# Weights' parts of a second MoE re-timed between blocks, and its first stores given to GpSimd

## The chip, the cores and the metric

The kernel runs on one core of one Trainium2 chip. The metric is the device time of one execution in microseconds. Engines are named as in the profile: PE is TensorE, DVE VectorE, ACT ScalarE, POOL GpSimd, SP SyncE; PEld is TensorE's loading of weights.

## The reference, cut to what matters

Three stages follow each other: a chunked local attention with memory tokens, a gated MoE, and a second MoE that sums four experts. The change lies in the second MoE:

```python
def _moe2_ref(x, domain_probs, w1, w2):          # x 1536x512, w1 4x512x1024, w2 4x1024x512
    p = domain_probs / (domain_probs.sum(-1, keepdims=True) + 1e-09)
    out = np.zeros((N, D), dtype=np.float32)
    for e in range(E):
        h = np.maximum(x @ w1[e], 0.0)
        out += p[:, e:e + 1] * (h @ w2[e])
    return out
```

## The kernel before, in words

**Numbers in two parts.** Matrices are multiplied as float32r in a high and a low part. ScalarE casts a matrix to its high part (`hi`, a copy), VectorE subtracts that from the matrix and gives the low part (`lo`), and `mm3` (lines 177 to 180) issues three matmuls: high by high, high by low, low by high.

**Seven products instead of eight.** In the second MoE both products, x by w1 and h by w2, are done on 2 x 2 quarters with seven products each and sums of quarters in between. So the weights of a group of half an expert's columns need four sums on VectorE (`s1` to `s4` for w1, `t4` to `t7` for w2, lines 282 and 327), seven casts on ScalarE (lines 272, 333) and seven low parts on VectorE (lines 278, 339). The sums overwrite the raw weights in place, so their order against casts and low parts is bound: a cast of a sum comes after it, and a sum that overwrites a quarter comes after the low part that reads it.

**Blocks.** There are eight groups (four experts, two halves each) and two halves of the tokens, so 16 blocks; blocks 2g and 2g+1 share group g's weights. Blocks 0 and 1 are plain in their second product (`plain_block`, `unit`, `o_part`): `flush` (line 546) scales a result on ScalarE (line 550) into one of four staging buffers `st`, and SP stores it plainly to the output (line 551), six stores of 256 KB per block. Blocks 2 to 15 (`block`) use seven products twice. Their results go through eight smaller buffers `st` and are added to the output by accumulating DMAs from GpSimd (line 662); `stage` (line 677, ScalarE), `second` (line 685, VectorE) and `c12` (line 694, ScalarE) read the results out of PSUM.

**The order of work.** The program is recorded in the order of the code (`manual_schedule`), and every engine takes its instructions in that order. In `block`, `product(n, u, m, ps, first)` is one of the seven products for unit u (six matmuls of 384 columns); `held` copies it to a small tile s on ScalarE (line 464), `total` adds two on VectorE (line 619, v<-a, v<-b, v<-e), the function `hi` makes the high part of h (lines 606, 608) and `lo` the low one (lines 613, 616), `s_sum` the sums of h (line 622), and `q` multiplies h with w2. The last third of each block's second products (`third`, `seventh`, `sixth`, `fourth`, `fifth`, in `left`) is run within the first third of the next block, between its products. `third(2)` adds to the PSUM tile B[2], which `fifth` has VectorE read (line 685) just before.

**Weights for the next group.** `w1_prep` and `w2_prep` return lists of steps. `block` puts them in `hooks` (lines 717 to 727), and `hook(n)` emits the next n steps at fixed places between products, so that a group's preparation is spread over the two blocks before it and the first of its own. In the lists a sum is followed by its cast and then by the cast's low part:

```python
        return [
            both(start, hi(1, "b11")), both(lo(1, "b11"), hi(2, "b21"), t5), both(lo(2, "b21"), t7),
            hi(7, "b12"), both(lo(7, "b12"), t6, hi(6, "b12")), both(lo(6, "b12"), t4, hi(4, "b21")),
            both(lo(4, "b21"), hi(5, "b11")), both(lo(5, "b11"), hi(3, "b22")),
            both(lo(3, "b22"), lambda: raw2_load(n + 1))]
```

**SP's queue** issues, in order, the loads of raw weights (lines 230, 239), the writes of y's seven parts to memory and their loads back (lines 370, 373, 768 KB each), and the plain stores (line 551).

Of the kernel before, what the change touches and what calls it, by code (L numbers as in the profile page):

```python
# [27 lines left out]
DM, DFF = 512, 1536  # L28
# [41 lines left out]
def fused_kernel(ctx: ExitStack, tc: tile.TileContext, kq0, kq1, kvw, kvc, vl, w_g, w_v, w_o, w_1, w_2, probs, out):  # L70
# [136 lines left out]
    raw1_t, raw2_t = [], []  # L207
# [50 lines left out]
    def w1_prep(n):  # L258

        t = {}  # L260

        def start():
            raw1_load(n)
            r0, r1 = raw1[n]
            t.update(a11=r0[:, :2], a12=r0[:, 2:], a21=r1[:, :2], a22=r1[:, 2:])
            ops1[n] = {}

        def hi(m, a):
            def do():
                s = slot("w")  # L270
                ops1[n][m] = s, quarters(s)
                nc.scalar.copy(out=ops1[n][m][1][:, 0], in_=t[a])
            return do

        def lo(m, a):
            def do():
                w = ops1[n][m][1]
                nc.vector.tensor_tensor(out=w[:, 1], in0=t[a], in1=f32(w[:, 0]), op=ALU.subtract)
            return do

        def comb(dst, a, b, op):
            return lambda: nc.vector.tensor_tensor(out=t[dst], in0=t[a], in1=t[b], op=op)


        s1 = comb("a22", "a21", "a22", ALU.add)
        s3 = comb("a21", "a11", "a21", ALU.subtract)
        s2 = comb("a11", "a22", "a11", ALU.subtract)
        s4 = comb("a12", "a12", "a11", ALU.subtract)
        return [
            both(start, hi(4, "a22"), hi(1, "a11")), both(lo(4, "a22"), s1),  # L290
            both(hi(2, "a12"), lo(1, "a11"), s3, s2), both(lo(2, "a12"), s4), hi(7, "a21"),
            both(hi(6, "a11"), lo(7, "a21")), lo(6, "a11"),
            both(hi(5, "a22"), hi(3, "a12")), lo(5, "a22"), both(lo(3, "a12"), lambda: raw1_load(n + 1))]
# [21 lines left out]

    def w2_prep(n):

        b = {}

        def start():  # L320
            raw2_load(n)
            r0, r1 = raw2s[n]
            b.update(b11=r0[:, :, :DH], b12=r0[:, :, DH:], b21=r1[:, :, :DH], b22=r1[:, :, DH:])
            ops3[n] = {}

        def comb(dst, x, y, op):
            return lambda: nc.vector.tensor_tensor(out=b[dst], in0=b[x], in1=b[y], op=op)

        def hi(m, x):
            def do():  # L330
                s = slot("w2")
                ops3[n][m] = s, quarters(s)
                nc.scalar.copy(out=ops3[n][m][1][:, :, 0], in_=b[x])  # L333
            return do

        def lo(m, x):
            def do():
                w = ops3[n][m][1]
                nc.vector.tensor_tensor(out=w[:, :, 1], in0=b[x], in1=f32(w[:, :, 0]), op=ALU.subtract)  # L339
            return do  # L340


        t5 = comb("b11", "b12", "b11", ALU.subtract)
        t7 = comb("b12", "b22", "b12", ALU.subtract)
        t6 = comb("b12", "b11", "b22", ALU.subtract)
        t4 = comb("b21", "b21", "b12", ALU.add)
        return [
            both(start, hi(1, "b11")), both(lo(1, "b11"), hi(2, "b21"), t5), both(lo(2, "b21"), t7),
            hi(7, "b12"), both(lo(7, "b12"), t6, hi(6, "b12")), both(lo(6, "b12"), t4, hi(4, "b21")),
            both(lo(4, "b21"), hi(5, "b11")), both(lo(5, "b11"), hi(3, "b22")),  # L350
            both(lo(3, "b22"), lambda: raw2_load(n + 1))]
# [76 lines left out]
    def second_block():  # L428
# [17 lines left out]
        def small(name, n):  # L446
            return sp.tile([128, HT], F32, tag=name, bufs=n, name=name)
# [897 lines left out]
```

## Time and profile before

| | |
|---|---|
| runs | 842.0, 843.4, 845.23 us (median 843.4) |
| the profiled execution | 843.81 us, its span 842.0 us |
| busy: PE | 827.6 us (98% of the span) |
| busy: PEld | 764.1 us (91%) |
| busy: DVE | 536.4 us (64%) |
| busy: ACT | 440.9 us (52%) |
| busy: POOL | 157.2 us (19%) |
| granted PE clock | 1.0 in every slice |
| chain that ended last | PE 65%, issue 16%, POOL 7%, DVE 5%, DMA 4%, ACT 3% |

The profiled execution's own time stands 1.8 us above its span, for what lies before the first and after the last instruction. Matmuls are pipelined, so that one starts while the one before is still running; PE's busy time is the union of them. The second MoE begins at about 345 us: plain blocks 0 and 1 take until about 410 us, and the other fourteen blocks about 30 us each. In the timelines a row with "xN" stands for N instructions in a row, and what stands in brackets is the idle time of the engine before it and what ended it.

### The profile page before, as it was taken

To read this page: it belongs to the slowest core of one execution; us is meant where nothing else is said; L and a number is where in the kernel's file an instruction comes from. 1 tells how busy PE (TensorE), PEld (TensorE's weight loads), DVE (VectorE), ACT (ScalarE), POOL (GpSimd) and SP (SyncE) were. 2 spreads that over 40 slices of the span, in tenths; PEclk is the share of its full clock that TensorE was granted. 3 is DMA by queue.
4 is the path that set the end of the run, shared out by engine and by line. 5 is a ranking of instruction groups with operands and counts; after the bars stand their busy time and mean duration, and the time that the engine had idled before them with its cause. 6 is when DMAs were issued, how large, how long until landed. Compare 5 with 4: busy or idle time off the path is not lost.

```text
span 842.0 us, 14479 instructions
## 1 busy us (share of the span) xinstructions
PE 827.6 (98%) x5566; PEld 764.1 (91%) x5566; DVE 536.4 (64%) x1041; ACT 440.9 (52%) x953; POOL 157.2 (19%) x182
## 2 busy tenths in 40 slices
PE   9999999999999999999999999999999999999998
PEld 6899998888888888888899999999999999999997
DVE  7753346342342229456588688788787787887847
ACT  5864454332232335445466666565665666666642
POOL 3220000000000000000032432333343243243231
PEclk9999999999999999999999999999999999999999
DMA  9984043111200005381593894893994994994783
GB/s 346 342 274 157 20 132 134 66 52 49 76 26 1 0 1 242 121 336 52 175 306 36 133 345 51 165 312 38 186 289 46 216 261 48 245 231 52 248 172 76
DMA packets 48614, 127.48 MB, mean 151 GB/s; under 512 B 5648, under 2 KB 27552, under 8 KB 48544
## 3 DMA queue, kind: packets, MB, share of 16 engines
q1 hardware_dynamic: 25616, 105.67, 34.8%
q0 software_dynamic: 22928, 20.88, 19.5%
q8 instruction: 44, 0.72, 0.3%
q14 instruction: 26, 0.21, 0.1%
HBM read 90.35 MB, written 36.18 MB: 150 GB/s over the span
## 4 chain that ended last, share of the span: by engine, by line
PE 65%; issue 16%; POOL 7%; DVE 5%; DMA 4%; ACT 3%; SPq 0%; POOLq 0%; ACTq 0%; DVEq 0%
POOL out_dram L662 7%; PE pv L178 4%; PE pv L180 4%; PE pv L179 4%; PE pg L179 4%; PE pg L178 4%; PE pb L178 4%; PE pb L179 4%; PE pb L180 4%; PE pg L180 4%; DMA out_dram<-st 3%; PE b L178 2%; PE b L179 2%; PE b L180 2%; PE B L178 2%
## 5 line engine op out<-in xcount | busy, mean ns | idle before, releaser
L662 POOL DMA_DIRECT2D out_dram<-st x159 | 137.3, 953 | 623.9 <-DVE st L685 599.1
L178 PE MATMUL b<-yo,w_s 128*128 128x384 f32 x256 | 87.2, 341 | 3.6 <-ACT s L464 2.9
L179 PE MATMUL b<-yo,w_s 128*128 128x384 f32 x256 | 86.5, 338 | 0.0
L180 PE MATMUL b<-yo,w_s 128*128 128x384 f32 x256 | 86.4, 337 | 0.0
L1086 ACT ACTIVATE sg<-pg 128x512 f32<-128x512 f32 x36 | 21.5, 598 | 84.2 <-PE pg L180 84.2
L622 DVE SCALAR_TENSOR_TENSOR v<-v 128x384 f32<-128x384 f32 x112 | 62.0, 553 | 4.6 <-ACT v L774 3.6
L178 PE MATMUL pv<-xs,w_v 128*128 128x384 f32 (+1 forms) x176 | 64.2, 365 | 0.0
L180 PE MATMUL pv<-xs,w_v 128*128 128x384 f32 (+1 forms) x176 | 61.7, 351 | 0.0
L179 PE MATMUL pv<-xs,w_v 128*128 128x384 f32 (+1 forms) x176 | 61.5, 349 | 0.0
L180 PE MATMUL pg<-xs,w_g 128*128 128x512 f32 x144 | 56.0, 389 | 0.0
L179 PE MATMUL pg<-xs,w_g 128*128 128x512 f32 x144 | 56.0, 389 | 0.0
L178 PE MATMUL pb<-hl,w_o 128*128 128x512 f32 x144 | 56.0, 389 | 0.0
L179 PE MATMUL pb<-hl,w_o 128*128 128x512 f32 x144 | 56.0, 389 | 0.0
L180 PE MATMUL pb<-hl,w_o 128*128 128x512 f32 x144 | 56.0, 389 | 0.0
L178 PE MATMUL pg<-xs,w_g 128*128 128x512 f32 x144 | 56.0, 389 | 0.0
L117 DVE TENSOR_TENSOR hl<-g,hl 128x512 fp32r<-128x512 f32 x36 | 24.7, 690 | 48.5 <-ACT hl L116 48.5
L464 ACT COPY s<-b 128x384 f32<-128x384 f32 x64 | 30.8, 481 | 46.1 <-PE b L180 44.6
L178 PEld LDWEIGHTS b<-yo,w_s 128*128 128x128 f32 x256 | 48.2, 188 | 6.1 <-ACT s L464 4.8
L178 PE MATMUL B<-w_s,h 128*128 128x256 f32 x171 | 48.9, 286 | 2.2 <-DVE st L685 2.2
L116 ACT CAST hl<-g 128x512 fp32r<-128x512 f32 x36 | 22.2, 623 | 54.8 <-PE pb L180 54.8
L339 DVE TENSOR_TENSOR w_s<-raw,w_s 128x512 fp32r<-128x512 f32 x49 | 33.7, 689 | 25.1 <-ACT w_s L333 25.1
L178 PE MATMUL B<-w_s,hx 128*128 128x256 f32 x165 | 47.0, 285 | 2.4 <-DVE st L685 2.4
(281 smaller groups left out, 2457.9 us busy)
## 6 DMA issues: line engine op xcount, KB each, us to landing
yo<-kept_y SPq DMA_DIRECT2D x49, 768.0 KB, 9.2
out_dram<-st POOLq DMA_DIRECT2D x159, 128.0 KB, 4.4
raw<-in_w_dram SPq DMA_DIRECT2D x32, 512.0 KB, 6.5
kept_y<-yo SPq DMA_DIRECT2D x14, 768.0 KB, 3.8
kv<-in_kvc_dram SPq DMA_DIRECT2D x20, 483.0 KB, 5.8
raw<-in_w_v_dram SPq DMA_DIRECT2D x12, 512.0 KB, 6.7
raw<-in_w_g_dram SPq DMA_DIRECT2D x12, 512.0 KB, 5.5
raw<-in_w_o_dram SPq DMA_DIRECT2D x12, 512.0 KB, 3.3
```

What stands on the lines that cost most here:

```text
L116: nc.scalar.copy(out=hi, in_=src)
L117: nc.vector.tensor_tensor(out=lo, in0=src, in1=f32(hi), op=ALU.subtract)
L178: nc.tensor.matmul(out=ps, lhsT=w_hi, rhs=r_hi, start=first, stop=False, skip_group_check=more)
L179: nc.tensor.matmul(out=ps, lhsT=w_hi, rhs=r_lo, start=False, stop=False, skip_group_check=more)
L180: nc.tensor.matmul(out=ps, lhsT=w_lo, rhs=r_hi, start=False, stop=last, skip_group_check=more)
L339: nc.vector.tensor_tensor(out=w[:, :, 1], in0=b[x], in1=f32(w[:, :, 0]), op=ALU.subtract)
L464: nc.scalar.copy(out=s, in_=ps[:, :HT])
L622: nc.vector.scalar_tensor_tensor(out=out, in0=x, scalar=0.0, in1=y, op0=ALU.max, op1=op)
L662: nc.gpsimd.dma_start(out=out_of(n, t, cols_of(dh)), in_=st, accum_op=ALU.add)
L1086: nc.scalar.activation(out=sg, in_=ps, func=AF.Sigmoid)
```

## The change

1. **Steps by name.** `w1_prep` and `w2_prep` now give a dictionary of single steps: "h4" is the cast of part 4, "l4" its low part, "s1" to "s7" the sums (s5, s7, s6, s4 are the former t5, t7, t6, t4), "x" the load of the next group's raw weights. `block` names at each place the steps to be emitted there, and `hooks` isn't used there any more.
2. **Order in a block.** In an even block l5, l3, x of w1 and l7, s6, s4 of w2 come after the first product, then the casts h6 and h4 with their low parts after product 7, the casts h5 and h3 alone between the next products, and l5 and l3 of w2 in mid-block (after product 3 of unit 0, and after product 7 of unit 1). In an odd block w1's first parts and sums stand as before, h1 and h2 of w2 are cast in the first third, and l1, then s5 and l2 come in mid-block. At the end of an odd block stand the casts h5 and h3 of w1, the sum s7 and the cast h7 of w2; at the end of an even block the casts h4, h1 and h2 of w1.
3. **`fifth` before a low part.** `do("5")` is called ahead of `lo(n, 0, 1, c11, True)` instead of behind it.
4. **Plain blocks.** In block 0 all four sums of y's second half come first, and `hook(2)` between the units is gone. In block 1 the cast h6 of w2 comes one step later (at the end of unit 1, behind s4).
5. **Plain stores.** `flush` issues its store on GpSimd's queue.

No instruction is added or left out; there are as many of each kind on PE, DVE and ACT.

```diff
+        def steps(of, sums):
+            do = {f"h{m}": hi(m, a) for m, a in of.items()}
+            do.update({f"l{m}": lo(m, a) for m, a in of.items()})
+            do.update({k: comb(*v) for k, v in sums.items()})
+            do["x"] = lambda: load(n + 1)
+            return do
...
+    def w1_do(g, steps):
+        if g < n_grp:
+            if g not in pre1:
+                pre1[g] = w1_prep(g)
+            for k in steps.split():
+                pre1[g][k]()
...
-            nc.sync.dma_start(out=out_of(n, tt, slice(0, DM)), in_=st)
+            nc.gpsimd.dma_start(out=out_of(n, tt, slice(0, DM)), in_=st)
...
-                thooks.extend(sums)
+                for do_sum in sums:
+                    do_sum()
             else:
-                env["w2"] = w2_prep(1)
-                thooks.extend(env["w2"][:6])
+                thooks.extend(each(w2_do, 1, "h1", "l1 h2 s5", "l2 s7", "h7", "l7 s6", "s4 h6", "l6 h4"))
             fin0 = unit(n, 0, prev)
-            if n == 0:
-                hook(2)
...
             product(n, 0, 1, b, True)
             s1 = held(b)
+            if odd:
+                w1_do(g + 1, "l4 s1 l1 s3 s2 l2 s4")
+            elif late:
+                w1_do(g, "l5 l3 x")
+                w2_do(g, "l7 s6 s4")
...
-            hook(2)
+            if odd:
+                w1_do(g + 1, "h7 l7 h6 l6")
+            else:
+                w2_do(g, "h6 l6 h4 l4" if late else "l4 h5 h3")
             product(n, 0, 6, b, False)
             s2 = held(b)
             do("6")
-            hook(2)
+            if odd:
+                w2_do(g + 1, "h1")
+            elif late:
+                w2_do(g, "h5")
...
             if late:
                 left["4"](E2)
+            if odd:
+                w2_do(g + 1, "h2")
+            elif late:
+                w2_do(g, "h3")
             product(n, 0, 5, b, False)
             total(b, s7, c22)
             hi(n, 0, 4, c22, True)
+            do("5")
             lo(n, 0, 1, c11, True)
-            do("5")
...
             left.clear()
-            hook()
+            w2_do(g + odd, "l1" if odd else "l5")
...
             s_sum(n, 0, 7)
+            w2_do(g + odd, "s5 l2" if odd else "l3 x")
             s_lo(n, 0, 5)
             s_hi(n, 0, 7)
-            hook()
...
                 stage(n, 1, tt, 1, E[tt])
+            if odd:
+                w1_do(g + 1, "h5 h3")
             s_lo(n, 1, 5)
...
             s_lo(n, 1, 3)
-            if odd == 0 and g + 1 < n_grp:
-                w1[0]()
+            if odd:
+                w2_do(g + 1, "s7")
+            else:
+                w1_do(g + 1, "h4 h1")
...
-            if odd == 0 and g + 1 < n_grp:
-                w1[1]()
+            if odd:
+                w2_do(g + 1, "h7")
+            else:
+                w1_do(g + 1, "h2")
```

**The order on VectorE, first third of block 10 (an even block).** w_s are the weights' parts, raw_1_2836 and raw_0_2834 the raw w1, raw_0_3291 and raw_1_3293 the raw w2; B_9 (with the tile's number) is block 9's B[2], which `fifth` reads. Before:

```order
L339 TENSOR_TENSOR w_s_3654<-raw_0_3291,w_s_3654 128x2x256
L327 TENSOR_TENSOR raw_0_3291<-raw_0_3291,raw_1_3293 128x2x256
L339 TENSOR_TENSOR w_s_3709<-raw_0_3291,w_s_3709 128x2x256
L327 TENSOR_TENSOR raw_1_3293<-raw_1_3293,raw_0_3291 128x2x256
L339 TENSOR_TENSOR w_s_3331<-raw_1_3293,w_s_3331 128x2x256
L619 TENSOR_TENSOR v<-a_0_6557,s 128x384
L685 SCALAR_TENSOR_TENSOR st_3296<-E_10_6512,p_sb,st_3296 128x256
L619 TENSOR_TENSOR v<-b_0_6485,s 128x384
L613 SCALAR_TENSOR_TENSOR h_0_3827<-v,h_0_3827 128x384
L685 SCALAR_TENSOR_TENSOR st_3296<-B_9_6399,p_sb,st_3296 128x256
L619 TENSOR_TENSOR v<-e_0_6515,s 128x384
L613 SCALAR_TENSOR_TENSOR h_1_3828<-v,h_1_3828 128x384
```
With the change:

```order
L269 TENSOR_TENSOR w_s_3706<-raw_0_3291,w_s_3706 128x2x256
L275 TENSOR_TENSOR raw_0_3291<-raw_0_3291,raw_1_3293 128x2x256
L275 TENSOR_TENSOR raw_1_3293<-raw_1_3293,raw_0_3291 128x2x256
L269 TENSOR_TENSOR w_s_3709<-raw_0_3291,w_s_3709 128x2x256
L269 TENSOR_TENSOR w_s_3334<-raw_1_3293,w_s_3334 128x2x256
L619 TENSOR_TENSOR v<-a_0_6557,s 128x384
L685 SCALAR_TENSOR_TENSOR st_3296<-E_10_6520,p_sb,st_3296 128x256
L619 TENSOR_TENSOR v<-b_0_6488,s 128x384
L685 SCALAR_TENSOR_TENSOR st_3296<-B_9_6398,p_sb,st_3296 128x256
L613 SCALAR_TENSOR_TENSOR h_0_3827<-v,h_0_3827 128x384
L619 TENSOR_TENSOR v<-e_0_6521,s 128x384
```
The second and third sum of raw w2 stand together ahead of the two low parts, and the reading of B_9 stands ahead of the low part of h_0.

**The order on VectorE, start of plain block 0.** yr are the two halves of y (the sums read the second and write into the first), h_0 the parts of h, w_s the parts of w2. Before:

```order
L248 TENSOR_TENSOR yr_2839<-yr_2840 128x2x384
L307 TENSOR_TENSOR w_s_3331<-raw_0_3291,w_s_3331 128x512
L490 TENSOR_TENSOR v<-a_0_3316,s 128x384
L490 TENSOR_TENSOR v<-e_0_3298,s 128x384
L485 SCALAR_TENSOR_TENSOR h_0_(0, 0)_3338<-v,h_0_(0, 0)_3338 128x384
L248 TENSOR_TENSOR yr_2839<-yr_2840 128x2x384
L490 TENSOR_TENSOR v<-b_0_3297,s 128x384
```
With the change:

```order
L248 TENSOR_TENSOR yr_2839<-yr_2840 128x2x384 x2
L248 TENSOR_TENSOR yr_2839<-yr_2840,yr_2839 128x2x384 x2
L338 TENSOR_TENSOR w_s_3334<-raw_0_3291,w_s_3334 128x512
L492 TENSOR_TENSOR v<-a_0_3319,s 128x384
L492 TENSOR_TENSOR v<-e_0_3302,s 128x384
L487 SCALAR_TENSOR_TENSOR h_0_(0, 0)_3341<-v,h_0_(0, 0)_3341 128x384
L492 TENSOR_TENSOR v<-b_0_3301,s 128x384
```
The four sums stand ahead of the first low part, and none is left between the low part of h and v<-b.

**The order on SP around the plain stores, before, and on GpSimd with the change.** st are the staging buffers, kept_y the writes of y's parts, raw the loads of weights. SP before:

```order
L370 DMA kept_y_79<-yo_2848 128x1536
L551 DMA out_dram<-st_3295 128x512 x2
L551 DMA out_dram<-st_3296 128x512 x2
L551 DMA out_dram<-st_3295 128x512 x2
L230 DMA raw_0_2834<-in_w_dram 128x1024
L230 DMA raw_1_2836<-in_w_dram 128x1024
L551 DMA out_dram<-st_3296 128x512 x2
L551 DMA out_dram<-st_3295 128x512 x2
```
GpSimd with the change:

```order
L158 TENSOR_TENSOR w_g_1141<-t_11_1101,w_g_1141 128x512
L553 DMA out_dram<-st_3295 128x512 x2
L553 DMA out_dram<-st_3296 128x512 x2
L553 DMA out_dram<-st_3295 128x512 x2
L553 DMA out_dram<-st_3296 128x512 x2
L553 DMA out_dram<-st_3295 128x512 x2
L553 DMA out_dram<-st_3296 128x512 x2
L662 DMA out_dram<-st_3295 128x256 x3
```
The twelve plain stores (128x512) have left SP's queue, where loads of weights and writes of y stand, and come first in GpSimd's, ahead of the accumulating ones (128x256).

## Rows read from the trace of the kernel before

**Rows 1.** Windows: busy us (instructions) of each engine, granted PE clock, DMA share, GB/s

```profile
410.00:842.00 432.00, 422.01 (x2945) 416.68 (x2943) 339.53 (x661) 258.47 (x555) 137.32 (x159) 1.00 0.73 175
...
815.00:842.00 27.00, 22.87 (x171) 22.67 (x169) 19.26 (x41) 8.94 (x20) 3.41 (x4) 1.00 0.34 70
```

**Rows 2.** Waits of TensorE, 345 to 842 us: us in total, times, longest

```profile
PE B L178 <- DVE st L685: 4.6, 12, 0.7
PE b L178 <- ACT s L464: 2.9, 3, 1.2
PE b L178 <- DVE v L490: 0.6, 1, 0.6
```

**Rows 3.** Timeline of PE, block 10: start, duration, operation, idle time before and releaser

```profile
660.74 0.34 PE L179 MATMUL e<-yo,w_s 128*128 128x384 f32 x1
660.91 0.34 PE L180 MATMUL e<-yo,w_s 128*128 128x384 f32 x1
661.64 0.39 PE L178 MATMUL B<-w_s,hx 128*128 128x256 f32 x1 [0.39 <-DVE st L685]
661.86 0.27 PE L179 MATMUL B<-w_s,hx 128*128 128x256 f32 x1
661.98 0.28 PE L180 MATMUL B<-w_s,hx 128*128 128x256 f32 x1
```

**Rows 4.** Timeline of DVE, block 10, up to its third part's reader

```profile
658.71 0.69 DVE L339 TENSOR_TENSOR w_s<-raw,w_s 128x512 fp32r<-128x512 f32 x1 [0.69 <-ACT w_s L333]
659.32 0.55 DVE L619 TENSOR_TENSOR v<-a,s 128x384 f32<-128x384 f32 x1
...
660.64 0.55 DVE L613 SCALAR_TENSOR_TENSOR h<-v,h 128x384 fp32r<-128x384 f32 x1
...
661.10 0.48 DVE L685 SCALAR_TENSOR_TENSOR st<-B,p_sb,st 128x256 f32<-128x256 f32 x1
```

**Rows 5.** Timeline of ACT, block 10

```profile
658.05 1.15 ACT L333 CAST w_s<-raw 128x512 fp32r<-128x512 f32 x2 [0.60 <-DVE raw L327]
```

**Rows 6.** Timeline of DVE, block 9

```profile
627.56 0.69 DVE L339 TENSOR_TENSOR w_s<-raw,w_s 128x512 fp32r<-128x512 f32 x1 [0.60 <-ACT w_s L333]
```

**Rows 7.** Timeline of PE, blocks 9 and 15

```profile
631.22 0.39 PE L178 MATMUL B<-w_s,hx 128*128 128x256 f32 x1 [0.73 <-DVE st L685]
...
640.13 0.34 PE L178 MATMUL b<-yo,w_s 128*128 128x384 f32 x1
...
813.46 0.29 PE L178 MATMUL B<-w_s,h 128*128 128x256 f32 x1
```

**Rows 8.** Timeline of DVE, block 9, unit 1

```profile
636.36 1.03 DVE L616 TENSOR_TENSOR h<-v,h 128x384 fp32r<-128x384 f32 x2 [1.32 <-ACT h L608]
...
638.91 0.56 DVE L619 TENSOR_TENSOR v<-b,s 128x384 f32<-128x384 f32 x1
```

**Rows 9.** Timeline of DVE, plain block 0

```profile
350.24 0.69 DVE L307 TENSOR_TENSOR w_s<-raw,w_s 128x512 fp32r<-128x512 f32 x1 [5.00 <-ACT w_s L301]
...
352.46 0.95 DVE L248 TENSOR_TENSOR yr<-yr 128x768 f32<-128x768 f32 x1
```

**Rows 10.** Timeline of ACT, plain blocks 0 and 1

```profile
378.90 0.69 ACT L550 ACTIVATE st<-d,p_sb 128x512 f32<-128x512 f32 x1 [5.78 <-DMA out_dram<-st]
...
390.86 0.62 ACT L333 CAST w_s<-raw 128x512 fp32r<-128x512 f32 x1 [1.10 <-DVE raw L327]
...
403.35 1.84 ACT L550 ACTIVATE st<-d,p_sb 128x512 f32<-128x512 f32 x3
...
413.19 0.69 ACT L550 ACTIVATE st<-d,p_sb 128x512 f32<-128x512 f32 x1 [6.81 <-PE d L180]
```

**Rows 11.** Timeline of SP's queue, plain block 1

```profile
406.59 8.99 SPq L551 DMA_DIRECT2D out_dram<-st  x6
```

**Rows 12.** Line 662 by itself: GpSimd's accumulating stores

```profile
L662 POOL DMA_DIRECT2D out_dram<-st x159: 841/855/1667, 430.7 to 828.2; - x159
...
DMA to landing us min/median/max: 2.9/4.4/11.1
```

More of the change, by code (lines that the diff above doesn't have):

```diff
@@ L256, in in_turn, with prepared @@
         return [his[0]] + [both(h, l) for h, l in zip(his[1:], los)] + [los[-1]]
[L258 to L266, printed above, removed]
+    def prepared(n, ops, tag, high, low, parts, load):
         def hi(m, a):
             def do():
-                s = slot("w")
-                ops1[n][m] = s, quarters(s)
-                nc.scalar.copy(out=ops1[n][m][1][:, 0], in_=t[a])
+                t = ops[n][m] = slot(tag)
+                nc.scalar.copy(out=high(t), in_=parts(n)[a])
             return do
@@ L276, in do @@
             def do():
-                w = ops1[n][m][1]
-                nc.vector.tensor_tensor(out=w[:, 1], in0=t[a], in1=f32(w[:, 0]), op=ALU.subtract)
+                t = ops[n][m]
+                nc.vector.tensor_tensor(out=low(t), in0=parts(n)[a], in1=f32(high(t)), op=ALU.subtract)
             return do
         def comb(dst, a, b, op):
-            return lambda: nc.vector.tensor_tensor(out=t[dst], in0=t[a], in1=t[b], op=op)
-        s1 = comb("a22", "a21", "a22", ALU.add)
-        s3 = comb("a21", "a11", "a21", ALU.subtract)
@@ L287, in w1_prep, with do @@
[L287 to L293, printed above, removed]
+            def do():
+                t = parts(n)
+                nc.vector.tensor_tensor(out=t[dst], in0=t[a], in1=t[b], op=op)
@@ new lines, in comb, with w1_prep, parts @@
+            return do
[4 more added lines that the diff above has]
+            do["x"] = lambda: load(n + 1)
+            return do
+        ops[n] = {}
+        return steps
+    def w1_prep(n):
+        def parts(n):
+            r0, r1 = raw1[n]
+            return dict(a11=r0[:, :2], a12=r0[:, 2:], a21=r1[:, :2], a22=r1[:, 2:])
+        raw1_load(n)
+        return prepared(n, ops1, "w", lambda t: quarters(t)[:, 0], lambda t: quarters(t)[:, 1], parts, raw1_load)(
+            {4: "a22", 1: "a11", 2: "a12", 7: "a21", 6: "a11", 5: "a22", 3: "a12"}, dict(
+                s1=("a22", "a21", "a22", ALU.add), s3=("a21", "a11", "a21", ALU.subtract),
+                s2=("a11", "a22", "a11", ALU.subtract), s4=("a12", "a12", "a11", ALU.subtract)))
@@ new lines, in w1_do, with each, w1_all, w2_prep @@
+    def w1_do(g, steps):
[4 more added lines that the diff above has]
+                pre1[g][k]()
+    def each(do, g, *steps):
+        return [lambda k=k: do(g, k) for k in steps]
+    def w1_all(g):
+        return each(
+            w1_do, g, "h4 h1", "l4 s1", "h2 l1 s3 s2", "l2 s4", "h7", "h6 l7", "l6", "h5 h3", "l5", "l3 x")
+    def w2_prep(n):
+        def parts(n):
+            r0, r1 = raw2s[n]
+            return dict(b11=r0[:, :, :DH], b12=r0[:, :, DH:], b21=r1[:, :, :DH], b22=r1[:, :, DH:])
+        raw2_load(n)
+        return prepared(n, ops3, "w2", lambda t: quarters(t)[:, :, 0], lambda t: quarters(t)[:, :, 1], parts, raw2_load)(
+            {1: "b11", 2: "b21", 7: "b12", 6: "b12", 4: "b21", 5: "b11", 3: "b22"}, dict(
+                s5=("b11", "b12", "b11", ALU.subtract), s7=("b12", "b22", "b12", ALU.subtract),
+                s6=("b12", "b11", "b22", ALU.subtract), s4=("b21", "b21", "b12", ALU.add)))
@@ L314, in w2_plain @@
         return [both(h[0], h[1], l[0]), both(h[2], l[1]), l[2], h[3], l[3]]
[L316 to L351, printed above, removed]
     def y_ops():
@@ L444, in hook, with w2_do @@
             emit(hooks, n)
+        def w2_do(g, steps):
+            if g < n_grp:
+                if g not in pre2:
+                    pre2[g] = w2_prep(g)
+                for k in steps.split():
+                    pre2[g][k]()
         def small(name, n):
```

29 lines of the change are left out of this document (8 added, 21 removed).

## The prediction

> **What bounds the kernel now.** I read the windows first: from 410 to 842 us, the second MoE's main part, TensorE is busy for 422.0 of 432 us [rows 1], so nothing but its waits can be won. It is short by 10.0 us, and 4.1 us of that is the tail after the last product, when results are stored [rows 1]. VectorE and ScalarE have 79% and 60% of that stretch, so neither is the bound by its sum; what counts is whether they are on time. The view of who waited for whom, from 345 us on, names 16 waits of TensorE [rows 2]: twelve of B for VectorE's line 685, 4.6 us, three of b for the copy to s, 2.9 us, one of b for v, 0.6 us. The reader should see in the timeline that the twelve are one per block, in blocks 3 to 14, at one place: the third part of the block before, which adds to B[2] after `fifth` has read it.
>
> A wait costs more than its idle time. Matmuls of 384 columns start 0.17 us apart but last 0.34, so an overlap of 0.17 is lost too; and the first one after a wait is followed after 0.22 us where the next pair is 0.12 apart [rows 3]. In block 10 the start was due at 660.91 + 0.17 and came at 661.64, 0.55 late, of which 0.39 is listed as idle. Each wait therefore costs its idle time plus 0.17 plus 0.10.
>
> **The change part by part.**
>
> *The twelve waits.* 4.6 + 12 x 0.27 = 7.8 us. Do they go? In an even block (10), VectorE's last low part waits 0.69 us for a cast [rows 4], and ScalarE made that cast only after 0.60 us of waiting for VectorE's sum [rows 5]: sums and casts hand the work back and forth, and v<-a follows at 659.32 with no idle time, so it stood ready behind them. The change issues both sums first and both casts afterwards, so that wait goes (0.69 us), and line 685 moves ahead of one line 613 (661.10 - 660.64 = 0.46 us). Together 1.15 us, against a lateness of 0.55. In an odd block (9) the first low part of w2 and its wait for a cast leave the place in front of v<-a, 0.69 + 0.60 us [rows 6], with the first sum of w2 behind it, and the 0.46 us comes on top: at least 1.75 us, against 0.73 + 0.17 = 0.90 of lateness [rows 7]. Block 15 has no weights to prepare and the old order of 613 and 685: its matmul at that place, 813.46, has no wait beside it [rows 7]. So a VectorE that comes on time is enough. Gain 7.8; the lower bound is that the reordering alone acts, 0.46 us of each lateness and its restart only where it covers it (about half, 3.9).
>
> *What the moved parts cost where they now stand.* The casts h5, h3 at the end of an odd block and h2 at the end of an even one lie on ScalarE, which has 40% of the stretch free. The sum s7 at the end of an odd block delays two lines 685 by 0.6 us; their readers come only after a whole product of the next block (6 x 0.17 = 1.0 us). In mid-block an odd block gets one sum and one low part (1.2 us of VectorE) ahead of line 616, where VectorE idles 1.32 us for a cast today [rows 8]; an even one moves a low part into the same gap. I take 0. Above it stands a small gain (an even block's low part no longer delays unit 1 from behind the first line 616), below it the price in the second rival.
>
> *Plain block 0.* The four sums of y (0.95 us each) now stand at its start, where VectorE idles 5.0 us before the first low part [rows 9]; they are hidden there, and if that cover were too short, the low part behind them would be late next. The sum at 352.46 no longer delays v<-b, so its wait goes: 0.56 + 0.27 = 0.8 us. One copy to s was 0.65 + 0.17 = 0.82 late behind two casts. It comes 0.87 earlier with v<-b and 0.53 earlier with one cast less (two casts take 1.15, one 0.62 [rows 5]), while TensorE comes 0.83 earlier: 0.82 - 1.40 + 0.83 = 0.25 and the 0.10 stay. Gain 0.8 + 0.9 - 0.35 = 1.4; bounds 0.8 and 1.7.
>
> *Plain block 1.* ScalarE's cast at 390.86 (h6) waits 1.10 us for a sum, and the copy to s that TensorE needs stands behind it [rows 10]. The change gives h6 one step later, after the unit's last product. Then the copy is earlier by the wait and the cast (1.10 + 0.62), more than the lateness of 1.17 + 0.17. That wait goes: gain 1.17 + 0.27 = 1.4.
>
> *The plain stores.* ScalarE's fifth scaled copy of each plain block waits 5.78 and 6.81 us [rows 10]. The first is listed as a wait for a store, the second for PE; there are four staging buffers and it is the fifth use, so I read both as the landing of the block's first store. In block 1 that store's data was ready at 403.35 + 0.69 = 404.0, but SP issues it at 406.59 behind two loads [rows 11]; in block 0 it stands behind seven writes of 768 KB. On GpSimd's queue nothing is ahead. A plain 256 KB store by GpSimd isn't in the trace; the nearest row is its accumulating one of 128 KB, 0.86 us to issue and 2.9, 4.4 or 11.1 us to land [rows 12]. I take the median: 404.0 + 0.86 + 4.4 = 409.3 instead of 413.2, which is earlier than TensorE needs the copy to s that follows. One wait of 1.12 + 0.27 = 1.4 goes; the copies and casts that now come closer together make the next one 0.1 longer. Gain 1.3. With the longest landing the fifth copy would come at 416.0, 2.8 later than today, and as much in block 0: a loss of 5.6 us.
>
> The trace has 159 such issues beside a VectorE that is busy for 79%: 841 ns at least, 1667 at most [rows 1, 12]. The Trainium skill (SBUF — State Buffer, "SBUF: two separate sides") speaks against this move: a DMA issued from GpSimd can starve, because VectorE in a two-port mode keeps GpSimd from writing descriptors; the page "SBUF — State Buffer" of the Trainium skill gives about 620 ns alone and 3100 overlapped. By that rule a store would land some 2.5 us later (an estimate from that page); no issue here takes even twice the shortest, so the trace does not bear it out, and I leave it to the first rival.
>
> **Sum:** 7.8 + 1.4 + 1.4 + 1.3 = 11.9 us. Against the profiled execution's own 843.81 this is 831.9; that execution stands 0.4 above the median of 843.4. Small waits may remain, so I don't subtract the 0.4: **832.0**.
>
> **The rivals.**
>
> *GpSimd is late with the plain stores.* In plain block 1 VectorE is in the middle of the next group's sums and low parts when the stores come. If the descriptors wait for it and landing takes the longest time shown, the store term is -5.6 instead of +1.3: 832.0 + 6.9 = 838.9. Against it: there are only 12 stores. Chance 0.04.
>
> *The mid-block parts make a new wait; slower than before.* Place: unit 1 of each block, where VectorE writes v<-b from 638.91 to 639.47 and product 3 starts at 640.13 [rows 7, 8], a slack of 0.66 us. VectorE takes its queue in order. If the two parts put in mid-block (0.61 each) also wait for their cast (0.62), VectorE is 1.84 us late, the gap of 1.32 not helping because the wait fills it, and each block costs 1.84 - 0.66 + 0.27 = 1.45 us. Twelve of them are 17.4: 832.0 + 17.4 = 849.4. From a lateness of 1.4 us per block on it is slower than before. For it: VectorE's 79%. Against it: the casts are given ahead of product 3 of unit 0, several products earlier. Chance 0.03.
>
> *Half of the twelve stay.* VectorE's work in the first third of a block is spread, not smaller, and ScalarE's stage copies can wait for a store ahead of h7 and h6. If only the reordering acts: 832.0 + 3.9 = 835.9. Block 15 speaks against it. Chance 0.13.
>
> *It doesn't do what it says.* A wait is put down to the last releaser, and the twelve could belong to something other than VectorE's queue; then only the plain blocks gain: 832.0 + 7.8 = 839.8. Rows 4 and 7 speak against it. Chance 0.03.
>
> **How the numbers follow.** The forecast has 0.77. Its own range, 829 to 835, is the spread of the runs before (842.0 to 845.2) around the sum, with the small terms at their ends. The range that leaves out less than 2 in 10 reaches to the half case with its own spread: 829.0 to 837.5. A measurement of this kernel tells about 0.5% (4.2 us) from no change; below 839.2 are the forecast, the half case and half of the late stores: 0.92. Within 0.5%: the other half and the last rival: 0.05. Slower: 0.03.
>
> **What would show it.** Right: no wait of B for line 685 in the view of waits, or a few under 0.2 us; two blocks together shorter by 1.3 us; the fifth scaled copy of each plain block directly behind its matmuls; VectorE's sums of block 0 before 349 us; in ScalarE's row h6 of block 1 behind the copy to s. Wrong: a new wait of b for v, or of A and E for h, in mid-block; GpSimd issues of 2 us or more; waits of ScalarE for stores in the later blocks.

## The result and the profile after

The changed kernel takes 831.34 us (median of 4 runs, 830.33 to 831.79), the kernel before 843.6 beside it (842.0 to 845.23): a ratio of 0.9853, interval 0.9832 to 0.9874. Predicted were 832.0, between 829.0 and 837.5. The profiled execution of after took 831.14 us, 12.67 less than that of before, and its span is 829.1.

The page of after, the engines' busy time and the chain of work that ended last by engine:

```profile
span 829.1 us, 14479 instructions
...
PE 823.2 (99%) x5566; PEld 764.9 (92%) x5566; DVE 541.4 (65%) x1041; ACT 441.0 (53%) x953; POOL 163.8 (20%) x194
...
PE 97%; DMA 1%; ACT 1%; DVE 1%; issue 0%; POOL 0%; SPq 0%; ACTq 0%; DVEq 0%; POOLq 0%
```

TensorE has 97% of the chain now; before, it had 65%. The windows of after (columns as in [rows 1]) for the plain blocks and for the rest up to the end:

```profile
344.80:409.00 64.20, 64.11 (x322) 57.64 (x321) 38.92 (x63) 35.69 (x66) 5.98 (x11) 1.00 0.43 164
...
410.00:829.00 419.00, 415.61 (x2929) 414.83 (x2928) 344.27 (x661) 256.63 (x552) 137.95 (x160) 1.00 0.73 177
```

TensorE leaves 3.4 of 419 us idle there (10.0 of 432 in [rows 1]). The view of waits has no row for TensorE between 340 and 842 us: all sixteen of [rows 2] are gone. Timeline of PE, blocks 9, 10 and 11, at the place of the twelve waits, where before 0.39 to 0.74 us of idle time stood:

```profile
622.37 0.34 PE L180 MATMUL e<-yo,w_s 128*128 128x384 f32 x1
622.54 0.28 PE L178 MATMUL B<-w_s,hx 128*128 128x256 f32 x1
622.66 0.28 PE L179 MATMUL B<-w_s,hx 128*128 128x256 f32 x1
...
652.31 0.28 PE L178 MATMUL B<-w_s,hx 128*128 128x256 f32 x1
...
682.09 0.28 PE L178 MATMUL B<-w_s,hx 128*128 128x256 f32 x1
```

The same place of block 11 in before:

```profile
692.40 0.39 PE L178 MATMUL B<-w_s,hx 128*128 128x256 f32 x1 [0.74 <-DVE st L685]
```

After, the product starts 0.17 us behind the last matmul of e and the next follows after 0.12: no wait, no loss behind it. Blocks 9 and 10 together take 682.09 - 622.54 = 59.55 us; before, from 631.22 [rows 7] to the same place of block 11, 692.40, they took 61.18. That is 1.6 less, where the prediction said 1.3, the mean of two waits; block 11's is the largest of the twelve.

To compare kernels without the noise of their start and end I use one stretch below: from the first product of plain block 0 to the start of the last addition of the block sums (line 666). Before it is 837.91 - 344.82 = 493.09 us, after 825.79 - 345.03 = 480.76, 12.33 less. Outside of it after begins the stretch 0.2 us later and ends 0.8 us sooner behind it (829.1 - 825.79 = 3.3 us against 4.1, the landing of the last stores); neither was edited. Together that is the 12.9 by which the spans differ.

### The profile page after: what moved, and what is told of

Same layout as the page of the kernel before. It is cut to its first block, busy times and chain, and to the rows that moved or that the text cites. A ratio compares the mean times of both kernels' runs of the same rounds, so it can differ in the third digit from the quotient of the medians.

```text
span 829.1 us, 14479 instructions
## 1 busy us (share of the span) xinstructions
PE 823.2 (99%) x5566; PEld 764.9 (92%) x5566; DVE 541.4 (65%) x1041; ACT 441.0 (53%) x953; POOL 163.8 (20%) x194
## 4 chain that ended last, share of the span: by engine, by line
PE 97%; DMA 1%; ACT 1%; DVE 1%; issue 0%; POOL 0%; SPq 0%; ACTq 0%; DVEq 0%; POOLq 0%
PE b L178 5%; PE b L179 5%; PE b L180 5%; PE B L180 5%; PE B L179 5%; PE B L178 5%; PE pv L178 4%; PE pv L180 4%; PE pv L179 4%; PE pg L180 4%; PE pg L178 4%; PE pb L180 4%; PE pb L178 4%; PE pb L179 4%; PE pg L179 4%; PE e L178 3%
## 5 line engine op out<-in xcount | busy, mean ns | idle before, releaser
L662 POOL DMA_DIRECT2D out_dram<-st x159 | 137.4, 929 | 267.6 <-DVE st L685 238.4
L269 DVE TENSOR_TENSOR w_s<-raw,w_s 128x512 fp32r<-128x512 f32 x105 | 69.4, 685 | 8.9 <-ACT w_s L263 8.9
L553 POOL DMA_DIRECT2D out_dram<-st x12 | 6.5, 543 | 337.2 <-ACT st L552 337.0
L263 ACT CAST w_s<-raw 128x512 fp32r<-128x512 f32 x105 | 61.1, 618 | 14.8 <-DVE raw L275 14.7
L178 PE MATMUL pv<-xs,w_v 128*128 128x384 f32 (+1 forms) x176 | 64.2, 365 | 0.0
L178 PEld LDWEIGHTS b<-yo,w_s 128*128 128x128 f32 x256 | 48.2, 188 | 1.3 <-ACT s L466 0.9
L179 PEld LDWEIGHTS b<-yo,w_s 128*128 128x128 f32 x256 | 48.2, 188 | 0.3
```

The costliest lines, as they stand in the source:

```text
L178: nc.tensor.matmul(out=ps, lhsT=w_hi, rhs=r_hi, start=first, stop=False, skip_group_check=more)
L179: nc.tensor.matmul(out=ps, lhsT=w_hi, rhs=r_lo, start=False, stop=False, skip_group_check=more)
L263: nc.scalar.copy(out=high(t), in_=parts(n)[a])
L269: nc.vector.tensor_tensor(out=low(t), in0=parts(n)[a], in1=f32(high(t)), op=ALU.subtract)
L553: nc.gpsimd.dma_start(out=out_of(n, tt, slice(0, DM)), in_=st)
L662: nc.gpsimd.dma_start(out=out_of(n, t, cols_of(dh)), in_=st, accum_op=ALU.add)
```

## The experiments

Theory: TensorE waits where an instruction stands too late in an in-order queue: line 685 in VectorE's for the twelve, a copy to s in ScalarE's for the plain blocks. Each edit acts by the lateness that it takes away, and anything beyond that is worth nothing. Rivals: the order of two calls did it alone; the moved parts did it alone; for the small terms, that they were covered anyway. Ratios are against the kernel before, run beside each.

**Only the order of two calls, on the kernel before**

```diff
-            lo(n, 0, 1, c11, True)
             do("5")
+            lo(n, 0, 1, c11, True)
```

> The kernel before with one edit: the call that emits the fifth pair of weight products for tile 2 (its VectorE addition is line 685) stands ahead of the call that makes the low part of c11 (line 613), instead of behind it; the weights' parts stay where they were. Theory of the late queue (TensorE waits for B because line 685 stands in VectorE's in-order queue behind what is late; before, the addition ends 0.32 to 0.91 us too late in blocks 3 to 14): one 0.55 us instruction fewer ahead of it removes ten of the twelve waits and leaves some 0.35 us and a restart in blocks 9 and 11, so about 838 us (836 to 839), two rows for line 685 among TensorE's waits. Theory 'the order alone': all twelve waits go, 835.8. Theory 'the moved parts alone' (the parts' new places did it, the order of these two calls is idle): no change, 843.6, twelve waits stay.

Measured 838.85 us, ratio 0.9935 (0.9909 to 0.9961); the stretch is 487.78, 5.31 shorter. Waits of TensorE, 340 to 842 us (columns as in [rows 2]):

```profile
PE b L178 <- ACT s L464: 3.1, 3, 1.3
PE B L178 <- DVE st L685: 0.6, 1, 0.6
PE b L178 <- DVE v L490: 0.6, 1, 0.6
```

One wait for line 685 is left of twelve, in block 11; elsewhere starts up to 0.24 us late remain, too short to be listed. The theory foresaw a second wait in block 9, which isn't there; the run with the odd blocks' parts back, below, shows what differs in these blocks. The gain is 5.3, against 5.6 by the theory, 7.8 by "the order alone" and none by "the moved parts alone".

**The changed kernel with that order undone**

```diff
-            do("5")
             lo(n, 0, 1, c11, True)
+            do("5")
```

> The changed kernel with that one edit undone: the fifth products' addition (line 685) stands behind the low part of c11 again, the parts stay in their new places. Theory of the late queue: VectorE is now early there by more than one 0.55 us instruction (in the changed kernel the block 9 addition ends at 622.17 and the products that want B start at 622.54), so the addition ends about 0.1 to 0.2 us late at worst: 831.3 to 833. 'The order alone': the twelve waits come back, 831.3 + 7.8 = 839. 'The moved parts alone': 831.3, no wait.

Measured 832.08, ratio 0.9854 (0.983 to 0.9877): the ratio of after. The stretch is 480.80, 0.04 more than after, and no wait is listed. Timeline of DVE, block 9:

```profile
621.42 0.55 DVE L613 SCALAR_TENSOR_TENSOR h<-v,h 128x384 fp32r<-128x384 f32 x1
621.89 0.47 DVE L685 SCALAR_TENSOR_TENSOR st<-B,p_sb,st 128x256 f32<-128x256 f32 x1
```

Line 685 ends at 622.36, and the product starts when it is due, at 622.52. So with the parts moved the order of the two calls is worth nothing, though alone on the kernel before it is worth 5.3. Each edit covers nearly the same lateness, and they don't add.

**The even blocks' parts back, and the odd blocks' parts back** (each with the order undone)

```diff
             elif late:
-                w1_do(g, "l5 l3 x")
-                w2_do(g, "l7 s6 s4")
+                w1_do(g, "h5 h3")
...
+                if not odd:
+                    w1_do(g, "l5")
+                    w2_do(g, "h7")
...
+            elif late:
+                w1_do(g, "l3 x")
+                w2_do(g, "l7 s6 h6")
             else:
-                w2_do(g, "h6 l6 h4 l4" if late else "l4 h5 h3")
+                w2_do(g, "l4 h5 h3")
...
-                w2_do(g, "h5")
+                w2_do(g, "l6 s4 h4 l4 h5")
...
-            if odd:
-                w1_do(g + 1, "h5 h3")
...
```

> The changed kernel with the order of those two calls undone and the parts of the even blocks 4 to 14 back where they stood before (casts h5 h3 of the first weight and h7 of the second again inside the block, their sums and low parts right behind them); odd blocks keep the new places. Late queue: six of the twelve waits come back, those of the even blocks (before they were 0.55 us late each, and about 0.1 us for the restart), some 3.9 us: 835.2 (834.5 to 836.5), and none in the odd blocks beyond those of the run with the order undone alone. 'The order alone': 839, the same as with the order alone undone. 'The moved parts alone': also about 835.2.

The odd blocks:

```diff
             if odd:
-                w1_do(g + 1, "l4 s1 l1 s3 s2 l2 s4")
+                w1_do(g + 1, "h2 l1 s3 s2")
...
+                if odd:
+                    w1_do(g + 1, "l2 s4")
...
-                w1_do(g + 1, "h7 l7 h6 l6")
+                w1_do(g + 1, "h7 h6 l7")
...
-                w2_do(g + 1, "h1")
+                w1_do(g + 1, "l6")
+                w2_do(g + 1, "h1 l1 h2 s5")
...
-            w2_do(g + odd, "l1" if odd else "l5")
+            if odd:
+                w2_do(g + 1, "l2")
+            else:
+                w2_do(g, "l5")
...
-                w1_do(g + 1, "h2")
+                w1_do(g + 1, "l4 s1")
```

As the last two lines show, l4 and s1 of w1 stood at the end of the even block before; the section on the change has them at their old place in the odd block, which is not so.

> The changed kernel with the order of those two calls undone and the first third and the middle of the odd blocks back as before (low parts l1 l2 and sum s5 of the second weight's group in the first third again instead of in mid-block, casts h2 and h4 h1 of the first weight's group where they stood, low part l4 and sum s1 at the end of the even block); even blocks keep the new places. Late queue: the waits of the odd blocks come back (0.32, 0.32, 0.50, 0.89, 0.91, 0.33 us before, and 0.10 each): 3.9 us, 835.2 (834 to 836.5), none in the even blocks. 'The order alone': 839. 'The moved parts alone': 835.2.

Even blocks back: 835.01, ratio 0.989 (0.9866 to 0.9913), stretch 484.58, 3.8 more than after. Odd blocks back: 835.27, ratio 0.9892 (0.9863 to 0.9921), stretch 485.66, 4.9 more. Waits of TensorE, 340 to 842 us, with the even blocks back:

```profile
PE B L178 <- DVE st L685: 2.3, 6, 0.4
```

With the odd blocks back:

```profile
PE B L178 <- DVE st L685: 3.0, 6, 1.1
```

Each kernel has six waits, every second block, and only in the blocks whose parts stand in the old places. "The order alone" (839 for both) falls. The odd blocks cost 1 us more than expected: in blocks 9 and 11 the start is 1.23 and 1.24 us late instead of 0.89 and 0.91. What these blocks have is a wait of line 677 for a store out of the buffers `st`, with casts behind it in ScalarE's queue. Timeline of ACT, blocks 9 and 11, before:

```profile
624.66 0.47 ACT L677 ACTIVATE st<-E,p_sb 128x256 f32<-128x256 f32 x1 [0.70 <-DMA out_dram<-st]
...
687.72 0.48 ACT L677 ACTIVATE st<-B,p_sb 128x256 f32<-128x256 f32 x1 [0.48 <-DMA out_dram<-st]
```

And with the odd blocks back:

```profile
618.86 0.48 ACT L677 ACTIVATE st<-E,p_sb 128x256 f32<-128x256 f32 x1 [1.14 <-DMA out_dram<-st]
...
681.54 0.48 ACT L677 ACTIVATE st<-B,p_sb 128x256 f32<-128x256 f32 x1 [0.75 <-DMA out_dram<-st]
```

In these two profiles an odd block without such a wait is 0.32 or 0.33 us late (only block 7 of before has 0.50 without a listed wait). In the run with the order alone, line 677 waits for no store in block 9, whose wait is gone, and longer than before in blocks 11 and 13 (0.75 and 0.62 us), which gain least. So a part of the odd blocks' lateness comes from the landing of earlier stores and changes from profile to profile. This is read from the rows; no edit tested it.

**The plain stores: back to SyncE in the changed kernel, and to GpSimd alone in the kernel before**

```diff
-            nc.gpsimd.dma_start(out=out_of(n, tt, slice(0, DM)), in_=st)
+            nc.sync.dma_start(out=out_of(n, tt, slice(0, DM)), in_=st)
```

> The changed kernel with the twelve plain stores given out by SyncE's queue again, all else as changed. If the stores' place is worth what the prediction gave it: 831.3 + 1.3 to 1.7 = 832.6 to 833.0, the fifth scaled copy of each plain block late again behind its store (before at 378.90 and 413.19 us; in the changed kernel 375.78 and 405.46) and two waits of TensorE behind it. If the plain stores were early enough by themselves once the rest is moved: 831.3, no wait.

The second is the same line the other way round.

> The kernel before with one edit: the twelve plain stores are given out by GpSimd's queue. By the prediction's term: 843.6 - 1.3 to 1.7 = 841.9 to 842.3, the copies of the fifth tiles earlier by about 3 and 7 us, the wait at 406.6 us gone and the twelve waits for line 685 still there. If the stores only gained together with the other edits: 843.6. If GpSimd's issues are late (2 us and more each): slower than 843.6.

Back to SyncE: 835.35, ratio 0.9891 (0.9877 to 0.9906), stretch 483.88, 3.1 more than after, which is twice what was expected. Timeline of SP's queue in that kernel, plain block 0:

```profile
370.58 9.54 SPq L553 DMA_DIRECT2D out_dram<-st  x5
```

Timeline of ACT, the fifth copy of each plain block, and in block 0 the copy behind it:

```profile
379.08 0.69 ACT L552 ACTIVATE st<-d,p_sb 128x512 f32<-128x512 f32 x1 [7.03 <-DMA out_dram<-st]
379.66 0.47 ACT L466 COPY s<-b 128x384 f32<-128x384 f32 x1
...
412.20 0.69 ACT L552 ACTIVATE st<-d,p_sb 128x512 f32<-128x512 f32 x1 [7.07 <-DMA out_dram<-st]
```

TensorE waits for that copy to s in both blocks, its start 1.47 and 1.55 us late.

To GpSimd in the kernel before: 842.9, ratio 0.9982 (0.9972 to 0.9993), that is 1.5 us (0.6 to 2.4), as expected; the stretch is 492.33, only 0.8 shorter. In its plain blocks 1.6 us are gained, and 0.9 are given back at two of the twelve waits, in blocks 11 and 13 (1.38 and 0.77 us late, before 0.91 and 0.33). In both of these blocks line 677 waits for a store in this profile (0.45 and 0.68 us), in block 13 of before it doesn't; no edit tested this.

The stores were thus worth 0.8 to 1.5 us by themselves and 3.1 us once the rest was done. SyncE gives them out from 370.58 us in this kernel and from 370.90 in the one before, and the fifth copy comes at 379.08 and 378.90: both hardly move, while TensorE, with block 0 shortened, reaches the place 1.1 us sooner (378.49 against 379.57). What block 0 gains would then be waited away at the store. The next run tests that.

**Only the edits of plain block 0, on the kernel before**

```diff
-                thooks.extend(sums)
+                for do_sum in sums:
+                    do_sum()
...
-            if n == 0:
-                hook(2)
```

> The kernel before with only the edits of plain block 0: the four sums of line 248 ahead of the block's first product instead of one by one inside it, and no two steps of weights' parts between its units; stores stay with SyncE, the other parts where they were. If the terms of the prediction simply add: 1.4 us less, 842.2, the two waits of 352 to 355 us gone and the wait at 379.6 us as before (0.22 us). If the stores hold what block 0 gains (SyncE begins to give the stores out at 370.6 to 370.9 us in either kernel, so the sixth tile's copy stays where it is while TensorE comes to it earlier): the start lost at 379 us grows from 0.22 to some 1.4 us and of the 1.4 us 0.2 to 0.4 are left, about 843.2.

Measured 843.98, ratio 1.0002 (0.9992 to 1.0013); the stretch is 492.90, 0.2 shorter: no gain. Timeline of ACT (its stretch begins 1.5 us later than before's, see the last section):

```profile
380.31 0.69 ACT L550 ACTIVATE st<-d,p_sb 128x512 f32<-128x512 f32 x1 [7.04 <-DMA out_dram<-st]
```

The idle time ahead of the fifth copy has grown from 5.78 [rows 10] to 7.04 us, and TensorE's start behind it is 1.47 late instead of 0.22. So the 1.4 us of block 0 are real only together with the stores.

**One part of each plain block back**

```diff
-                for do_sum in sums:
-                    do_sum()
+                thooks.extend(sums)
```

> The changed kernel with the sums of the next activations (line 248) of plain block 0 handed out one by one inside the block again, as before. By the prediction's term for block 0 (two waits of TensorE for VectorE's additions at 350 to 353 us, 0.8 and 0.9 us less a remainder of 0.35): 831.3 + 1.4 = 832.7. If the sums are covered wherever they stand: 831.3.

```diff
-                thooks.extend(each(w2_do, 1, "h1", "l1 h2 s5", "l2 s7", "h7", "l7 s6", "s4 h6", "l6 h4"))
+                thooks.extend(each(w2_do, 1, "h1", "l1 h2 s5", "l2 s7", "h7", "l7 s6 h6", "l6 s4 h4"))
```

> The changed kernel with the list of the second weight's parts in plain block 1 as it was before: cast h6 and cast h4 each one step earlier, h6 ahead of the copy to s. By the prediction's term for block 1: 831.3 + 1.4 = 832.7, with one wait of TensorE near 390 us behind ScalarE's copy. If the cast is covered: 831.3.

Sums back: 833.27, ratio 0.9868 (0.9849 to 0.9887), stretch 481.68, 0.9 more than after: one wait of 0.56 us for v<-b is back and costs its 0.84; the second start is 0.28 late, as in after (0.25), since the moved casts stay moved. List back: 833.32, ratio 0.9868 (0.9851 to 0.9885), stretch 482.23, 1.5 more, with this in the timeline of ACT:

```profile
389.52 0.62 ACT L263 CAST w_s<-raw 128x512 fp32r<-128x512 f32 x1 [1.11 <-DVE raw L275]
...
390.43 0.47 ACT L466 COPY s<-b 128x384 f32<-128x384 f32 x1
```

The cast h6 waits 1.11 us for its sum with the copy to s behind it, as in [rows 10]. "Covered" falls for both. The intervals of these two overlap that of after, so here the stretch and the rows decide, not the times.

**How much more mid-block takes: one low part, then two**

```diff
-                w1_do(g + 1, "h7 l7 h6 l6")
+                w1_do(g + 1, "h7 l7 h6")
...
+            if odd:
+                w1_do(g + 1, "l6")
             w2_do(g + odd, "s5 l2" if odd else "l3 x")
```

With two, the lists are "h7 h6" and "l7 l6".

> The changed kernel with one more low part in mid-block: in the odd blocks 3 to 13 the first weight's part l6 (0.68 us on VectorE) moves from the first third to the place ahead of the sum s5 and the low part l2. Theory of the late queue: VectorE's addition that product 3 of the second unit wants (in the changed kernel it ends at 630.70 in block 9, the products start at 631.36, 0.66 us of room) ends about 0.5 to 0.7 us later, which the room just takes: 831.3, at most 0.3 more. Rival 'no room in mid-block': every one of the six blocks pays 0.68 and a restart of 0.1, 831.3 + 4.7 = 836.0.

> The same with two low parts moved, l7 and l6 of the first weight (1.36 us of VectorE in mid-block of six odd blocks). Late queue: some 1.2 us later against 0.66 us of room, so a new wait of about 0.55 us and 0.1 for the restart in six blocks: 831.3 + 3.9 = 835.2 (834.3 to 836.5), rows of waits of b for line 619 in mid-block, none for line 685. Rival 'VectorE has room everywhere' (it is busy 65% of the span): 831.3. Rival 'no room': 831.3 + 6 x 1.46 = 840.

One: 831.04, ratio 0.9851 (0.9838 to 0.9865), stretch 480.80, nothing. Two: 833.89, ratio 0.9885 (0.9871 to 0.9898), stretch 482.33, 1.57 more (in the profiled execution another 1.4 us lie ahead of the stretch, see the last section). Timeline of DVE with two, block 9:

```profile
628.35 1.28 DVE L269 TENSOR_TENSOR w_s<-raw,w_s 128x512 fp32r<-128x512 f32 x2
629.55 0.68 DVE L275 TENSOR_TENSOR raw<-raw 128x512 f32<-128x512 f32 x1
...
633.10 0.55 DVE L619 TENSOR_TENSOR v<-b,s 128x384 f32<-128x384 f32 x1
```

Timeline of PE beside it:

```profile
633.43 0.28 PE L180 MATMUL B<-w_s,h 128*128 128x256 f32 x1
633.70 0.44 PE L178 MATMUL b<-yo,w_s 128*128 128x384 f32 x1
633.98 0.34 PE L179 MATMUL b<-yo,w_s 128*128 128x384 f32 x1
```

The edge is there: v<-b ends at 633.65 and the product that was due at 633.55 starts at 633.70, 0.15 late (too little for a row in the view of waits), and the next follows after 0.28 instead of 0.17. That is 0.26 us in each of six blocks, 1.56 in all. It is less than the 0.65 per block expected: two parts are issued 0.60 apart, not 0.68, and idle times of VectorE in front (the one before line 616 among them, 0.15 in after) take up part of it. Both rivals fall: VectorE doesn't have room everywhere, and mid-block has some.

**The three casts that still stand in the way**

```diff
-        return [both(h[0], h[1], l[0]), both(h[2], l[1]), l[2], h[3], l[3]]
+        return [both(h[0], h[1], l[0]), l[1], h[2], both(l[2], h[3]), l[3]]
...
-                thooks.extend(each(w2_do, 1, "h1", "l1 h2 s5", "l2 s7", "h7", "l7 s6", "s4 h6", "l6 h4"))
+                thooks.extend(each(w2_do, 1, "h1", "l1 h2 s5", "l2 s7", "", "h7 l7 s6", "s4 h6", "l6 h4"))
...
-                w2_do(g, "h6 l6 h4 l4" if late else "l4 h5 h3")
+                w2_do(g, "h6 l6 h4 l4" if late else "l4")
...
-            elif late:
-                w2_do(g, "h5")
+            else:
+                w2_do(g, "h5" if late else "h5 h3")
```

> The changed kernel with the three casts that still stand ahead of a wanted copy to s moved behind it: in plain block 0 the third cast one step later, in plain block 1 cast h7 one step later, in block 2 casts h5 and h3 behind the copy of product 6. Late queue: the starts lost at 354.3, 388.0 and 412.0 us (0.25, 0.16 and 0.31 us, with 0.11 us for each restart) go, 831.3 - 1.0 = 830.3 (829.8 to 831.0). Rival 'the moved casts make another copy late': 831.3 or more, with a new row at the next copy to s.

Measured 830.69 (829.93 to 830.77), ratio 0.9844 (0.983 to 0.9857). The stretch is 479.80, 0.96 shorter than after, and the three late starts are gone. It has the lowest time of this study, but its interval overlaps that of after: the gain is shown by the rows, not by the times.

## Why the prediction was right

*The sum.* Each term of it shows in the starts that TensorE lost, counted as the prediction did (distance of two starts, less the usual one). The twelve: 6.6 us late and 1.2 behind them before, nothing after, 7.8 as predicted. Block 0: 1.76 before, 0.36 after, 1.40 (predicted 1.4, with 0.35 left). Block 1: 1.79 and 0.37, 1.42 (predicted 1.4). The stores: 2.02 and 0.42, 1.6 (predicted 1.3; the 0.3 more is the start in block 0 that was 0.21 late, with its restart, which the prediction left out). The forecast holds, and the price of a wait (its idle time, 0.17 and 0.10) is confirmed.

*Why the twelve went: the step was right, its reason only half.* The prediction let the wait of 0.69 us for a cast ahead of v<-a [rows 4] go. The last low part has no wait of its own any more, but the one in front of it has. Timeline of DVE after, block 10:

```profile
642.83 1.89 DVE L269 TENSOR_TENSOR w_s<-raw,w_s 128x512 fp32r<-128x512 f32 x3
644.75 1.42 DVE L275 TENSOR_TENSOR raw<-raw,raw 128x512 f32<-128x512 f32 x2
647.20 1.29 DVE L269 TENSOR_TENSOR w_s<-raw,w_s 128x512 fp32r<-128x512 f32 x2 [1.02 <-ACT w_s L263]
648.97 0.56 DVE L619 TENSOR_TENSOR v<-a,s 128x384 f32<-128x384 f32 x1 [0.49 <-PE a L180]
...
651.46 0.48 DVE L685 SCALAR_TENSOR_TENSOR st<-B,p_sb,st 128x256 f32<-128x256 f32 x1 [0.16 <-PE B L180]
651.87 0.55 DVE L613 SCALAR_TENSOR_TENSOR h<-v,h 128x384 fp32r<-128x384 f32 x1
```

There is a wait of 1.02 us for casts ahead of the last two low parts. What went is the handing back and forth as a whole. The same stretch of before, block 10:

```profile
652.85 1.29 DVE L278 TENSOR_TENSOR w_s<-raw,w_s 128x512 fp32r<-128x512 f32 x2 [1.64 <-ACT w_s L272]
654.62 0.69 DVE L339 TENSOR_TENSOR w_s<-raw,w_s 128x512 fp32r<-128x512 f32 x1 [0.48 <-ACT w_s L333]
655.35 0.69 DVE L327 TENSOR_TENSOR raw<-raw,raw 128x512 f32<-128x512 f32 x1
656.73 0.69 DVE L339 TENSOR_TENSOR w_s<-raw,w_s 128x512 fp32r<-128x512 f32 x1 [0.69 <-ACT w_s L333]
```

With the last one in [rows 4] VectorE idled 1.64 + 0.48 + 0.69 + 0.69 = 3.50 us for casts there. The largest, 1.64, was for casts made inside the block; with them in the block in front, the first three low parts start at once. Now v<-a waits for TensorE (0.49 us here, 0.36 in the odd block 9), no longer TensorE for VectorE. The prediction looked only at the last wait of the row and so gave 0.46 of its 1.15 us to the order of the two calls; the runs show that this order is worth nothing beside the moved parts.

*"The reordering alone, about half, 3.9"* was added up wrongly. By its own rule, 0.46 us of each lateness and the restart where that covers it, the twelve latenesses of before (0.32 to 0.91 us) give 5.4, and the run measured 5.3. The rival in which half of the twelve stay would have stood at 834.4 instead of 835.9.

*The stores, 1.3,* were taken as a term of their own. By themselves they bring 0.8 to 1.5, taken away last they cost 3.1: block 0's 1.4 hides behind them. The sum held because all edits were made at once. The fifth copy of block 1 was forecast for 409.3 us; it comes at 405.46 and waits for TensorE, not for a store. Timeline of ACT after, both plain blocks:

```profile
375.78 0.69 ACT L552 ACTIVATE st<-d,p_sb 128x512 f32<-128x512 f32 x1 [3.85 <-DMA out_dram<-st]
...
405.46 0.69 ACT L552 ACTIVATE st<-d,p_sb 128x512 f32<-128x512 f32 x1 [2.03 <-PE d L180]
```

In block 0 the fifth copy still waits 3.85 us for the first store, but is early enough. "Directly behind its matmuls" was right for block 1 only. The landing was taken as 4.4 us, from stores of another kind. Line 553 after, in block 0 and then in block 1:

```profile
DMA to landing us min/median/max: 3.9/7.8/8.9
...
DMA to landing us min/median/max: 2.3/4.0/7.1
```

Line 551 before, in block 0:

```profile
DMA to landing us min/median/max: 2.0/6.4/7.9
```

So in block 0 a store from GpSimd's queue takes no less time to land than one from SyncE's; it is issued sooner, from 368.2 us instead of 370.9. The 4.4 fits block 1 alone, where the one wait stood that the term counts.

*The rivals.* GpSimd late: no. Line 553 and line 662 of after, by themselves:

```profile
L553 POOL DMA_DIRECT2D out_dram<-st x12: 539/539/580, 368.2 to 411.3; - x12
...
L662 POOL DMA_DIRECT2D out_dram<-st x159: 842/857/1677, 426.6 to 815.9; - x159
...
DMA to landing us min/median/max: 2.9/4.6/11.2
```

No issue takes even twice the shortest, as before [rows 12], with VectorE busy for 82% of the stretch of line 662 (344.27 of 419 us) and for 61% of the plain blocks (38.92 of 64.2 us). The starving that the Trainium skill warns of ("SBUF — State Buffer", "SBUF: two separate sides") doesn't show. That page of the Trainium skill speaks of VectorE in a two-port mode; whether VectorE is in one here, no run shows. Of the queues that the Trainium skill advises there instead, ScalarE's and SyncE's, SyncE's costs 3.1 us here, and ScalarE's wasn't tried. A new wait in mid-block: no, but it was one low part away; the slack of 0.66 us in the prediction is there in after too (v<-b ends at 630.70, the product starts at 631.36). Half of the twelve stay: no; that happens when half of the blocks get their old places back. One of the signs of being wrong is there all the same: line 677 of after waits for a store three times, 0.9 us in all (before twice, 1.2 us). It costs TensorE nothing, since VectorE is no longer late behind it. It doesn't do what it says: no.

## What to carry to other kernels

When an engine waits for the tail of another engine's in-order queue, add up every idle time in that queue up to the point that is waited for, not the last one; casts made one block ahead remove the handing over, and any further reordering there is then worth nothing. Terms don't add: edits that cure the same lateness count once (5.3 alone, 0 as the last), and a gain ahead of a transfer that starts at a fixed time counts only once that transfer is moved (0.2 alone). An instruction that nobody waits for can be moved at no cost until the slack beside it (0.66 us here) is used up, and the first edge is cheap (0.26 us per block).

## What the runs showed of the hardware

*TensorE's clock at the start of a kernel.* In two runs (two low parts in mid-block, block 0 alone) the stretch begins at 346.4 us instead of 344.6 to 345.6, though nothing ahead of it was edited. Timeline of PE at the start, after:

```profile
5.63 0.84 PE L984 MATMUL s<-kv 128*128 128x16 f32 x6
6.32 0.97 PE L964 MATMUL warm<-zero 128*128 128x384 bf16 x5
7.40 0.78 PE L982 MATMUL s<-kv 128*32 128x112 f32 x24
```

And with two low parts in mid-block:

```profile
5.85 1.46 PE L986 MATMUL s<-kv 128*128 128x16 f32 x6
7.15 1.76 PE L966 MATMUL warm<-zero 128*128 128x384 bf16 x5
...
10.09 0.84 PE L986 MATMUL s<-kv 128*128 128x16 f32 x6
```

The same five matmuls take 0.97 us in one and 1.76 in the other, about half the speed, as at 1.2 instead of 2.4 GHz. The six matmuls of s take 1.46 us at 5.85 there and 0.84 at 10.09, as after has them at 5.63 already, while the granted clock reads 1.00 in both. The same instructions ran before it in both kernels. The Trainium skill ("TensorE: Matmul & The Clock Gate", "Part 1: The HAM clock gate") says that the number of slow matmuls at a kernel's start differs between runs of one kernel; these rows fit that, but whether it is the run or the program wasn't separated. It makes up to 1.5 us, as much as one term of the sum, which is why the stretch was compared and not the span.

*Plain stores by GpSimd are issued faster than accumulating ones*: 539 ns at 256 KB against 842 to 1677 at 128 KB.
